# A fused attention and gated feed-forward kernel: the feed-forward's order, its bias and its place among the attention visits

## The chip, the cores and the metric

The kernel runs on one core of one Trainium2 chip. The metric is the device time in microseconds of one execution, the median of several. The profile is one such execution, taken by the hardware profiler; its span runs from the first to the last instruction. The engines are TensorE (PE; its weight loads, PEld, overlap its matmuls), VectorE (DVE), ScalarE (ACT), GpSimd (POOL) and SyncE (SP), whose queue issues most of the DMA transfers here.

## The reference

Eight batches of grouped attention (16 query heads, 4 key heads, 384 positions, head size 64) are followed by a feed-forward with a spatial gate, on each batch's 384 x 1024 attention output.

```python
scores = scale * np.matmul(q, k.transpose(0, 1, 3, 2))
attn = np.exp(scores); attn = attn / (np.sum(attn, axis=-1, keepdims=True) + 1e-09)
x = np.matmul(attn, v)                       # then heads side by side: (8, 384, 1024)
h = np.maximum(x @ w_in, 0.0)                # 1024 -> 1024
u, v = h[..., :512], h[..., 512:]
v_n = (v - mean(v)) / np.sqrt(var(v) + 1e-06)
v_s = np.einsum('ts,bsd->btd', w_spatial, v_n) + b_spatial[None, :, None]
out = (u * v_s) @ w_out                      # 512 -> 1024
```

The bias b_spatial has one value per position t, the same for all 512 channels.

## The kernel before, in words

Matmul operands are fp16, sums are fp32 in PSUM. The 384 positions are three tiles of 128; position s sits in tile s % 3, so that loads are contiguous.

**Attention in visits.** The outer loop (L456) runs over batches b = 0 to 8, the inner one over nine visits vi. Each visit computes two score units (scores, L260; unit u is one 128 x 1024 piece, two matmuls for two heads of 64 rows each, 18 units a batch), and ScalarE takes the exp of each unit into aT (L281). Two PSUM buffers of two banks hold scores, so the scores of one visit wait for the exps of the visit before. At four of the visits (VALUES_AT, L430: visit 0 for the batch before, visits 3, 5 and 8 for the batch itself) values (L285) computes the sums of the exps, their reciprocal on ScalarE (Ln, then Exp with scale -1, L307 and L308), and two pieces X of attention times v, each multiplied by the reciprocal on VectorE into xT (L312). So xT of batch b is complete after visit 0 of batch b+1.

**Feed-forward in pieces.** feed_forward(b) (L418) lists pieces of TensorE work, each with a cost in microseconds that the planner uses: mk_v three times (eight matmuls of 512 columns, relu on ScalarE into v_r, statistics on VectorE; the third also computes rstd on ScalarE and the three v_n on VectorE), mk_u four times (eight matmuls of 384 columns into a transposed U, relu on VectorE into uT, L371), mk_sp four times (a matmul of the bias rows, L380, and three matmuls of v_n with the transposed spatial weights, L382; VectorE multiplies by uT into gT, L389), and mk_out six times (four matmuls of 512 columns, a copy on VectorE, L410; every second one a store of 512 KB, L412).

**The bias as a matmul.** load_bias (L165) splits the 384 biases into an fp16 high part and an fp16 rest, in rows 0 and 32 of bias_rows; bias_ones has ones in these two rows. Their product adds the bias to every channel with fp32-like accuracy.

**The planner.** The pieces of batch b-1 are queued at visit 2 of batch b (L478), or all at once when b is 8 (the tail). In each visit a budget grows by per_visit, the cost of a batch's pieces and four values calls over nine visits, and pieces are taken from the queue while less has been done than the budget allows (L486). In a middle batch that gives V, V, V at visit 2; U at 3; U, U at 4; U at 5; the four spatial pieces at 6; three out at 7, one at 8, two at visit 0 of the next batch; none at visit 1. For the first batch three transposes of the spatial weights (transpose_ws, L209) are put in ahead of the spatial pieces.

**What fixes the order.** TensorE, GpSimd and SyncE run in the order in which the program is written (manual_schedule, L437); VectorE's and ScalarE's order is chosen by the framework's scheduler when the kernel is built. Each engine works in order. One PSUM pool of four banks (ps, L73) is shared in turn by all pieces but the scores: sums, X, V, U, spatial and out. SyncE's queue carries the loads of the next batch (issued in visit 2), the DMA transposes of k and q (visits 6 and 8, after GpSimd's casts to fp16), and the out stores, in the written order.

Of the kernel before, what the change touches and what calls it, by code (L numbers as in the profile page):

```python
# [10 lines left out]
FP32 = mybir.dt.float32  # L11
FP16 = mybir.dt.float16
# [6 lines left out]
def kernel(  # L19
# [20 lines left out]
    P = 128  # L40
# [105 lines left out]
    ident16 = cst.tile([P, P], FP16, name="ident16")  # L146
    ones32 = cst.tile([P, 32], FP16, name="ones32")
    eps_t = cst.tile([P, 1], FP32, name="eps_t")
    bias_rows = cst.tile([P, S], FP16, name="bias_rows")
    bias_ones = cst.tile([P, P], FP16, name="bias_ones")  # L150
    w_in16 = wpool.tile([P, NKT, DFF], FP16, name="w_in16")
    w_out16 = wpool.tile([P, NDT, DM], FP16, name="w_out16")
    wsT16 = wpool.tile([P, NST, S], FP16, name="wsT16")
# [1 line left out]
    def load_consts():  # L155
        make_identity(nc, ident)
        nc.vector.tensor_copy(ident16, ident)  # L157
        nc.vector.memset(ones32, 1.0)
        nc.vector.memset(eps_t, eps_ln)
        nc.vector.memset(bias_rows, 0.0)  # L160
        nc.vector.memset(bias_ones, 0.0)
        nc.vector.memset(bias_ones[0:1, :], 1.0)
        nc.vector.memset(bias_ones[32:33, :], 1.0)

    def load_bias():  # L165
        b32 = cst.tile([1, S], FP32, name="b32")
        lo32 = cst.tile([1, NST, P], FP32, name="lo32")
        nc.sync.dma_start(b32, moe_b_spatial.rearrange("(a s) -> a s", a=1))
        b_tp = b32.rearrange("a (p t) -> a t p", t=NST)
        hi = bias_rows[0:1, :].rearrange("a (t p) -> a t p", t=NST)  # L170
        lo = bias_rows[32:33, :].rearrange("a (t p) -> a t p", t=NST)
        nc.vector.tensor_copy(hi, b_tp)
        nc.vector.tensor_tensor(lo32, b_tp, hi, ALU.subtract)
        nc.vector.tensor_copy(lo, lo32)

    def load_w_in(c0, c1):

# [31 lines left out]
    def transpose_ws(st):  # L209
        ws16 = loaded["ws16"]  # L210
        psw = ps.tile([P, NST, P], FP16, name=f"psw_{st}", tag="ps")
        for tt in range(NST):
            nc.tensor.transpose(psw[:, tt, :], ws16[:, tt, st, :], ident16)
        nc.vector.tensor_copy(wsT16[:, st, :].rearrange("p (t q) -> p t q", t=NST), psw)
# [104 lines left out]
    def mk_v(b, st):  # L319
        def f():  # L320
            xt = xT[b]
            if st == 0:
                held["mv", b] = small.tile([P, NST, 2], FP32, name=f"mv_{b}", tag="mv")
            mv = held["mv", b]
            pv = ps.tile([P, 512], FP32, name=f"pv_{b}_{st}", tag="ps")
            for kc in range(NKT):
                nc.tensor.matmul(  # L327
                    pv,
                    xt[:, kc, st * P : (st + 1) * P],
                    w_in16[:, kc, DH:DFF],  # L330
                    start=(kc == 0),
                    stop=(kc == NKT - 1),
                )
            v_r = moe_v.tile([P, DH], FP32, name=f"v_r_{b}_{st}", tag="v_r")
            nc.scalar.activation(v_r, pv, AF.Relu)
            stats = small.tile([P, 6], FP32, name=f"stats_{b}_{st}", tag="stats")
            nc.vector.bn_stats(stats, v_r)
            nc.vector.bn_aggr(mv[:, st, :], stats)  # L338
            held["v_r", b, st] = v_r
            if st == NST - 1:  # L340
                rstd = small.tile([P, NST], FP32, name=f"rstd_{b}", tag="rstd")
                nc.scalar.activation(rstd, mv[:, :, 1], AF.Ln, bias=eps_t)
                nc.scalar.activation(rstd, rstd, AF.Exp, scale=-0.5)
                for s2 in range(NST):
                    v_n = moe_v.tile([P, DH], FP16, name=f"v_n_{b}_{s2}", tag="v_n")
                    nc.vector.tensor_scalar(
                        v_n,
                        held["v_r", b, s2],
                        mv[:, s2, 0:1],
                        rstd[:, s2 : s2 + 1],  # L350
                        op0=ALU.subtract,
                        op1=ALU.mult,
                    )
                    held["v_n", b, s2] = v_n

        return f

    def mk_u(b, mu):
        def f():
            if mu == 0:  # L360
                held["uT", b] = moe_sb.tile([P, NDT, S], FP16, name=f"uT_{b}", tag="uT")
            pu = ps.tile([P, 512], FP32, name=f"pu_{b}_{mu}", tag="ps")
            for kc in range(NKT):
                nc.tensor.matmul(  # L364
                    pu[:, 0:S],
                    w_in16[:, kc, mu * P : (mu + 1) * P],
                    xT[b][:, kc, :],
                    start=(kc == 0),
                    stop=(kc == NKT - 1),
                )  # L370
            nc.vector.tensor_scalar(held["uT", b][:, mu, :], pu[:, 0:S], 0.0, None, op0=ALU.max)  # L371

        return f

    def mk_sp(b, m):
        def f():
            if m == 0:
                held["gT", b] = moe_sb.tile([P, NDT, S], FP16, name=f"gT_{b}", tag="gT")
            psp = ps.tile([P, 512], FP32, name=f"psp_{b}_{m}", tag="ps")
            nc.tensor.matmul(psp[:, 0:S], bias_ones, bias_rows, start=True, stop=False)  # L380
            for st in range(NST):
                nc.tensor.matmul(  # L382
                    psp[:, 0:S],
                    held["v_n", b, st][:, m * P : (m + 1) * P],
                    wsT16[:, st, :],
                    start=False,
                    stop=(st == NST - 1),
                )
            nc.vector.tensor_tensor(  # L389
                held["gT", b][:, m, :], psp[:, 0:S], held["uT", b][:, m, :], ALU.mult  # L390
            )

        return f
# [23 lines left out]

    def feed_forward(b):  # L418

        return (  # L420
            [(1.72, mk_v(b, st)) for st in range(NST)]
            + [(1.30, mk_u(b, mu)) for mu in range(NDT)]
            + [(0.66, mk_sp(b, m)) for m in range(NDT)]
            + [(0.87, mk_out(b, tt, h)) for tt in range(NST) for h in range(2)]
        )


# [9 lines left out]
    with tc.manual_schedule(engines={PE, POOL, SP}):  # L437
        load_k(0)
        load_q(0, 0, pieces=2)
        cast_k(0, nc.vector)  # L440
        cast_q(0, 0, nc.vector)
        load_v(0)
        load_q(0, 1, pieces=2)
        cast_v(0, nc.gpsimd)
        cast_q(0, 1, nc.gpsimd)
        load_w_in(DH, DFF)
        load_w_in(0, DH)
        load_w_out()
        transpose_k(0)
        transpose_q(0, 0, 0)  # L450
        transpose_q(0, 0, 1)

        total = sum(t for t, _ in feed_forward(0))
        per_visit = (total + 4 * T_VALUES) / VISITS
        budget = 0.0
        for b in range(B + 1):  # L456
            for vi in range(VISITS if b < B else 1):
                if b < B:
                    scores(b, [2 * vi, 2 * vi + 1])
                if vi in VALUES_AT:  # L460
                    db, gp, quad = VALUES_AT[vi]
                    if 0 <= b + db < B and (b < B or db < 0):
                        values(b + db, gp, quad)
                        done += T_VALUES
                if b < B:
                    if b == 0 and vi in (1, 2):
                        transpose_q(b, 1, vi - 1)
                    if vi == 2 and b + 1 < B:
                        load_batch(b + 1, nc.vector if b == 0 else nc.gpsimd)
                    if vi == 6 and b + 1 < B:  # L470
                        dma_transpose_k(b + 1)
                        dma_transpose_q(b + 1, 0)
                    if vi == 8 and b + 1 < B:
                        dma_transpose_q(b + 1, 1)
                    if b == 0 and vi == 3:
                        load_ws()
                        load_bias()
                if vi == 2 and b > 0 or b == B:  # L478
                    queue += feed_forward(b - 1)
                    if b == 1:  # L480
                        queue[7:7] = [(0.2, lambda st=st: transpose_ws(st)) for st in range(NST)]
                if b == 0:
                    done = budget = 0.0
                    continue
                budget += per_visit
                while queue and (b == B or done < budget):  # L486
                    t, f = queue.pop(0)
                    f()
                    done += t
                if not queue:  # L490
                    done = max(done, budget - per_visit)
# [30 lines left out]
```

## Time and profile before

The median of three runs is 290.3 us (289.22 to 290.8). The profiled execution took 289.11 us with a span of 287.3 us, mean granted TensorE clock 0.979.

| stretch of the span (us) | what | length |
|---|---|---|
| 0 to 41.17 | first batch's attention, weights loaded, to the first V matmul | 41.17 |
| 41.17 to 74.68 | first V to second V | 33.51 |
| 74.68 to 235.35 | five middle periods: 32.13, 31.82, 31.83, 32.55, 32.34 | 160.67 |
| 235.35 to 264.28 | last attention visits | 28.93 |
| 264.28 to 287.3 | tail: the last batch's feed-forward and last store | 23.02 |

A stretch between two V matmuls holds one batch of steady work. In the answers of the trace, x after a group is its number of instructions, and an arrow in square brackets names what ended an engine's idle time and how long that was. DMA transfers are busy for 53.6% of 16 engines' span on SyncE's queues and 7.9% on GpSimd's. Duration columns of matmuls overlap, since matmuls are pipelined: the spacing of their starts is what one costs.

### The profile page before, as it was taken

Reading aid. Unit: us, or ns where it says so; the run is one execution under the profiler, and the core shown is the slowest. Engines: PE = TensorE matmul, PEld = TensorE weight load, DVE = VectorE, ACT = ScalarE, POOL = GpSimd, SP = SyncE. Lnnn points to the kernel's source line nnn. Section 1 sums busy time; section 2 is a strip of 40 time slices with the busy share of each in tenths; the row PEclk is TensorE's granted clock in tenths of the full one; section 3 lists DMA queues with packets and bytes.
Section 4 is the critical chain, followed back from the end, with each engine's and each line's share of the span. In section 5 each row is a group of like instructions: output and inputs, shape, how many; then the busy total and the mean of one; then the engine's idle time right before and its main releaser. Section 6 shows DMA issues by size and latency. Waiting matters only on the chain.

```text
span 287.3 us, 5420 instructions
## 1 busy us (share of the span) xinstructions
PE 255.2 (89%) x2247; PEld 113.3 (39%) x2247; DVE 143.8 (50%) x277; ACT 184.4 (64%) x249; POOL 54.0 (19%) x88
## 2 busy tenths in 40 slices
PE   0685879989899989999899989999899989999993
PEld 0431234444344334444344434443344434444551
DVE  3427116474365443574365434674365434575673
ACT  1485895757676686758676776658676786664300
POOL 0654870600140004200150003300150000000000
PEclk9998599999999999999999999999999999999998
DMA  7999999906691479709790549406790530003105
GB/s 215 331 252 124 147 142 216 287 20 198 203 260 29 112 157 312 108 0 203 227 248 13 130 160 329 70 2 202 241 245 2 128 148 0 2 29 121 73 0 219
DMA packets 59402, 42.42 MB, mean 148 GB/s; under 512 B 29041, under 2 KB 55666, under 8 KB 59378
## 3 DMA queue, kind: packets, MB, share of 16 engines
q1 hardware_dynamic: 56274, 38.94, 53.6%
q0 software_dynamic: 3104, 3.15, 7.9%
q8 instruction: 17, 0.28, 0.4%
q14 instruction: 7, 0.06, 0.1%
HBM read 25.76 MB, written 12.58 MB: 133 GB/s over the span
## 4 chain that ended last, share of the span: by engine, by line
PE 75%; ACT 11%; DMA 6%; DVE 4%; issue 1%; SPq 1%; POOL 0%
DMA ws_318<-in_moe_w_spatial_dram 4%; DMA q_0_1_136<-in_q_dram 3%; ACT aT_1_337 L281 1%; ACT aT_0_2652 L281 1%; ACT aT_0_2216 L281 1%; ACT aT_0_471 L281 1%; ACT aT_0_1780 L281 1%; ACT aT_0_1344 L281 1%; ACT aT_0_3088 L281 1%; ACT aT_0_908 L281 1%; ACT aT_1_3288 L281 1%; ACT aT_1_686 L281 1%; SPq L106 1%; DVE ws_320 L204 1%; PE pv_0_3166 L327 1%
## 5 line engine op out<-in xcount | busy, mean ns | idle before, releaser
L364 PEld LDWEIGHTS <-w_in_107 128*128 128x128 f16 x256 | 23.4, 98 | 22.8 <-issue 8.8
L188 POOL DMA_DIRECT2D w_in_107<-in_moe_w_in_dram x32 | 17.2, 544 | 8.1 <-DMA w_in_107<-in_moe_w_in_dram 8.1
L296 PEld LDWEIGHTS <-ones_103 128*32 128x32 f16 x384 | 7.4, 97 | 15.8 <-issue 14.1
L238 PE MATMUL pk_178<-ident_102,k_0_128 128*128 128x128 f16 x6 | 0.8, 303 | 8.4 <-DVE ident_102 L157 8.4
L281 ACT ACTIVATE aT_0_210<-sc_0_204 128x1024 f16<-128x1024 f32 x1 | 1.0, 1023 | 9.1 <-PE sc_0_204 L268 9.1
L268 PEld LDWEIGHTS <-kT_185 64*128 64x128 f16 x36 | 2.1, 103 | 10.9 <-issue 10.8
L116 POOL CAST k_5_1861<-k_5_1857 128x384 f16<-128x384 f32 x2 | 1.0, 507 | 24.3 <-DMA k_5_1857<-in_k_dram 24.3
L116 POOL CAST k_6_2297<-k_6_2293 128x384 f16<-128x384 f32 x2 | 1.0, 507 | 24.1 <-DMA k_6_2293<-in_k_dram 24.1
L116 POOL CAST k_4_1425<-k_4_1421 128x384 f16<-128x384 f32 x2 | 1.0, 508 | 23.5 <-DMA k_4_1421<-in_k_dram 23.5
L116 POOL CAST k_7_2733<-k_7_2729 128x384 f16<-128x384 f32 x2 | 1.0, 508 | 23.4 <-DMA k_7_2729<-in_k_dram 23.4
L296 PEld LDWEIGHTS <-v_0_139 128*32 128x32 f16 x96 | 3.2, 122 | 5.0 <-issue 4.2
L116 POOL CAST k_3_989<-k_3_985 128x384 f16<-128x384 f32 x2 | 1.0, 507 | 20.6 <-DVE mv_1004 L338 20.6
L380 PEld LDWEIGHTS <-bias_ones 128*128 128x128 f16 x32 | 3.1, 97 | 4.3 <-issue 2.7
L204 DVE CAST ws_320<-ws_318 128x384 f16<-128x384 f32 x3 | 1.9, 672 | 5.7 <-DMA ws_318<-in_moe_w_spatial_dram 5.7
L238 PEld LDWEIGHTS <-k_0_128 128*128 128x128 f16 x6 | 0.6, 133 | 8.3 <-DVE k_0_128 L116 4.6
L312 DVE TENSOR_TENSOR xt_273<-X_1_0_0_435,rec_1_0_432 128x384 f16<-128x384 f32 x1 | 0.6, 558 | 6.5 <-ACT rec_1_0_432 L308 6.5
L327 PEld LDWEIGHTS <-xt_3225 128*128 128x128 f16 x24 | 2.4, 98 | 2.8
L403 PEld LDWEIGHTS <-gT_3644 128*128 128x128 f16 x24 | 2.3, 98 | 3.0 <-DVE gT_3644 L389 0.5
L327 PEld LDWEIGHTS <-xt_624 128*128 128x128 f16 x24 | 2.3, 98 | 2.8 <-issue 0.2
L327 PEld LDWEIGHTS <-xt_2808 128*128 128x128 f16 x24 | 2.3, 98 | 2.8 <-issue 0.2
L327 PEld LDWEIGHTS <-xt_2372 128*128 128x128 f16 x24 | 2.3, 98 | 2.8 <-issue 0.2
L327 PEld LDWEIGHTS <-xt_273 128*128 128x128 f16 x24 | 2.3, 98 | 2.8 <-issue 0.2
(1077 smaller groups left out, 755.9 us busy)
## 6 DMA issues: line engine op xcount, KB each, us to landing
w_in_107<-in_moe_w_in_dram POOLq DMA_DIRECT2D x32, 64.0 KB, 5.4
w_out_108<-in_moe_w_out_dram POOLq DMA_DIRECT2D x2, 512.0 KB, 7.8
q_0_0_125<-in_q_dram SPq DMA_DIRECT2D x2, 384.0 KB, 4.9
q_0_1_136<-in_q_dram SPq DMA_DIRECT2D x2, 384.0 KB, 7.5
q_1_0_248<-in_q_dram SPq DMA_DIRECT2D x1, 768.0 KB, 6.6
q_1_1_258<-in_q_dram SPq DMA_DIRECT2D x1, 768.0 KB, 8.5
q_2_0_536<-in_q_dram SPq DMA_DIRECT2D x1, 768.0 KB, 7.7
q_2_1_546<-in_q_dram SPq DMA_DIRECT2D x1, 768.0 KB, 7.8
```

The lines of the kernel that those rows point to most:

```text
L106: nc.sync.dma_start(q32[:, i * n : (i + 1) * n, :], q[b, h0 : h0 + n].rearrange("h (p t) d -> p h (t d)", t=NST),)
L116: engine.tensor_copy(k16[:, gp], k32[:, gp])
L188: nc.gpsimd.dma_start(w_in16[32 * i : 32 * (i + 1), kc : kc + 2, c0:c1], rows[jq])
L204: nc.vector.tensor_copy(ws16[:, tt, :, :], ws32[:, tt, :].rearrange("p (s t) -> p t s", t=NST))
L238: nc.tensor.transpose(pk[:, gp, t, :], k16[:, gp, t, :, :].rearrange("p h d -> p (h d)"), ident16,)
L268: nc.tensor.matmul(sc[:, half, :], kT[b][lo:hi, gp, t, :], rhs[lo:hi, c * 512 : (c + 1) * 512], start=True, stop=True,)
L281: nc.scalar.activation(aT[b, gp][:, t, :, c * 512 : (c + 1) * 512], sc, AF.Exp, scale=scale)
L296: nc.tensor.matmul(dst[32 * i : 32 * (i + 1), 0:S], weights(t, half), a[:, t, half, j * S : (j + 1) * S], start=(t == 0), stop=(t == NST - 1),
L327: nc.tensor.matmul(pv, xt[:, kc, st * P : (st + 1) * P], w_in16[:, kc, DH:DFF], start=(kc == 0), stop=(kc == NKT - 1),)
L364: nc.tensor.matmul(pu[:, 0:S], w_in16[:, kc, mu * P : (mu + 1) * P], xT[b][:, kc, :], start=(kc == 0), stop=(kc == NKT - 1),)
L380: nc.tensor.matmul(psp[:, 0:S], bias_ones, bias_rows, start=True, stop=False)
L403: nc.tensor.matmul(po, gT[:, m, tt * P : (tt + 1) * P], w_out16[:, m, half * 512 : (half + 1) * 512], start=(m == 0), stop=(m == NDT - 1),)
```

## The change

The feed-forward's order becomes V, out of the batch before, spatial, U; the last batch's own out follows at the end. Spatial no longer needs U: it writes v_s with the bias added, in fp32, on VectorE, from a bias that a DMA has laid out over all 128 partitions (bias_b). U's evacuation then does relu and the product with v_s in one VectorE instruction, straight into gT. So the bias matmul, the bias rows and uT go; v_s (fp32) comes. Out of batch b-1 takes U's place between V and spatial, as work for TensorE while VectorE and ScalarE normalise V. The pieces are queued from visit 1 on instead of visit 2, and the planner's total becomes 17.58 instead of 18.22. The batch of the first feed-forward has no earlier out; it gets the three small transposes of the spatial weights in that place.

```diff
-    bias_rows = cst.tile([P, S], FP16, name="bias_rows")
-    bias_ones = cst.tile([P, P], FP16, name="bias_ones")
+    bias_b = cst.tile([P, S], FP32, name="bias_b")
...
-        nc.vector.memset(bias_rows, 0.0)
-        nc.vector.memset(bias_ones, 0.0)
-        nc.vector.memset(bias_ones[0:1, :], 1.0)
-        nc.vector.memset(bias_ones[32:33, :], 1.0)
 
     def load_bias():
...
-        nc.sync.dma_start(b32, moe_b_spatial.rearrange("(a s) -> a s", a=1))
...
-        nc.vector.tensor_copy(hi, b_tp)
-        nc.vector.tensor_tensor(lo32, b_tp, hi, ALU.subtract)
-        nc.vector.tensor_copy(lo, lo32)
+        nc.sync.dma_start(bias_b, moe_b_spatial.partition_broadcast(P))
...
+    def mk_sp(b, m):
+        def f():
+            if m == 0:
+                held["v_s", b] = moe_sb.tile([P, NDT, S], FP32, name=f"v_s_{b}", tag="v_s")
+            psp = ps.tile([P, 512], FP32, name=f"psp_{b}_{m}", tag="ps")
+            for st in range(NST):
+                nc.tensor.matmul(
+                    psp[:, 0:S],
+                    held["v_n", b, st][:, m * P : (m + 1) * P],
+                    wsT16[:, st, :],
+                    start=(st == 0),
+                    stop=(st == NST - 1),
+                )
+            nc.vector.tensor_tensor(
+                held["v_s", b][:, m, :].rearrange("p (t s) -> p t s", t=NST),
+                psp[:, 0:S].rearrange("p (t s) -> p t s", t=NST),
+                bias_b.rearrange("p (s t) -> p t s", t=NST),
+                ALU.add,
+            )
...
     def mk_u(b, mu):
...
-            nc.vector.tensor_scalar(held["uT", b][:, mu, :], pu[:, 0:S], 0.0, None, op0=ALU.max)
...
-            nc.tensor.matmul(psp[:, 0:S], bias_ones, bias_rows, start=True, stop=False)
...
-            nc.vector.tensor_tensor(
-                held["gT", b][:, m, :], psp[:, 0:S], held["uT", b][:, m, :], ALU.mult
-            )
+            nc.vector.scalar_tensor_tensor(
+                held["gT", b][:, mu, :],
+                pu[:, 0:S],
+                0.0,
+                held["v_s", b][:, mu, :],
+                op0=ALU.max,
+                op1=ALU.mult,
+            )
...
     def feed_forward(b):
 
+        last = [(0.87, mk_out(b - 1, tt, h)) for tt in range(NST) for h in range(2)] if b else []
+        own = [(0.87, mk_out(b, tt, h)) for tt in range(NST) for h in range(2)] if b == B - 1 else []
         return (
             [(1.72, mk_v(b, st)) for st in range(NST)]
+            + (last or [(0.2, lambda st=st: transpose_ws(st)) for st in range(NST)])
+            + [(0.50, mk_sp(b, m)) for m in range(NDT)]
             + [(1.30, mk_u(b, mu)) for mu in range(NDT)]
-            + [(0.66, mk_sp(b, m)) for m in range(NDT)]
-            + [(0.87, mk_out(b, tt, h)) for tt in range(NST) for h in range(2)]
+            + own
         )
...
-        total = sum(t for t, _ in feed_forward(0))
+        total = sum(t for t, _ in feed_forward(1))
...
-                if vi == 2 and b > 0 or b == B:
+                if vi == 1 and b > 0 or b == B:
                     queue += feed_forward(b - 1)
-                    if b == 1:
-                        queue[7:7] = [(0.2, lambda st=st: transpose_ws(st)) for st in range(NST)]
```

More of the change, by code (lines that the diff above doesn't have):

```diff
@@ L159, in load_consts @@
         nc.vector.memset(eps_t, eps_ln)
-        nc.vector.memset(bias_rows, 0.0)
-        nc.vector.memset(bias_ones, 0.0)
-        nc.vector.memset(bias_ones[0:1, :], 1.0)
-        nc.vector.memset(bias_ones[32:33, :], 1.0)
     def load_bias():
-        b32 = cst.tile([1, S], FP32, name="b32")
-        lo32 = cst.tile([1, NST, P], FP32, name="lo32")
-        nc.sync.dma_start(b32, moe_b_spatial.rearrange("(a s) -> a s", a=1))
[L169 to L172, printed above, removed]
-        nc.vector.tensor_tensor(lo32, b_tp, hi, ALU.subtract)
-        nc.vector.tensor_copy(lo, lo32)
+        nc.sync.dma_start(bias_b, moe_b_spatial.partition_broadcast(P))
     def load_w_in(c0, c1):
@@ L356, in mk_v @@
         return f
+    def mk_sp(b, m):
[17 more added lines that the diff above has]
+            )
+        return f
     def mk_u(b, mu):
@@ L360, in f @@
             if mu == 0:
-                held["uT", b] = moe_sb.tile([P, NDT, S], FP16, name=f"uT_{b}", tag="uT")
+                held["gT", b] = moe_sb.tile([P, NDT, S], FP16, name=f"gT_{b}", tag="gT")
             pu = ps.tile([P, 512], FP32, name=f"pu_{b}_{mu}", tag="ps")
@@ L370, in f @@
                 )
-            nc.vector.tensor_scalar(held["uT", b][:, mu, :], pu[:, 0:S], 0.0, None, op0=ALU.max)
[L373 to L387, printed above, removed]
-                )
-            nc.vector.tensor_tensor(
-                held["gT", b][:, m, :], psp[:, 0:S], held["uT", b][:, m, :], ALU.mult
+            nc.vector.scalar_tensor_tensor(
[5 more added lines that the diff above has]
+                op1=ALU.mult,
             )
```

## The prediction

> **What bounds the kernel now.** First the page's busy rows and the chain that ended last.
>
> ```profile
> PE 255.2 (89%) x2247; PEld 113.3 (39%) x2247; DVE 143.8 (50%) x277; ACT 184.4 (64%) x249; POOL 54.0 (19%) x88
> PE 75%; ACT 11%; DMA 6%; DVE 4%; issue 1%; SPq 1%; POOL 0%
> ```
>
> TensorE is busy 89% of the span and is 75% of the chain; ScalarE is 11% of it. So a matmul removed is time removed, as long as ScalarE isn't waited for. I cut the span at the first V matmul of each batch (their starts are in the chain) and asked for busy time per stretch; three of the eight:
>
> ```profile
> 41.17:74.68 33.51, 31.32 (x286) 14.04 (x287) 17.19 (x34) 23.02 (x32) 4.92 (x7) 1.00 0.77 172
> 106.81:138.63 31.82, 30.40 (x277) 13.38 (x278) 16.14 (x31) 22.85 (x32) 4.93 (x7) 1.00 0.66 155
> 264.28:287.30 23.02, 18.33 (x97) 9.12 (x94) 13.09 (x24) 2.29 (x5) 0.00 (x0) 0.96 0.23 94
> ```
>
> Columns: stretch and length, then PE, PEld, DVE, ACT, POOL, clock, DMA. A middle batch lasts 31.82 us. VectorE (16.14) and ScalarE (22.85) have room over a whole batch; the lost time must be local. The timeline around a batch's first V matmul shows where:
>
> ```profile
> 103.99 0.39 PE L268 MATMUL sc_2_1405<-qT_0_1221,kT_1219 64*128 64x512 f16 x2
> 104.42 1.02 ACT L281 ACTIVATE aT_0_1344<-sc_2_1405 128x1024 f16<-128x1024 f32 x1 [1.07 <-PE sc_2_1405 L268]
> 105.34 1.02 ACT L281 ACTIVATE aT_0_1344<-sc_3_1408 128x1024 f16<-128x1024 f32 x1
> 105.50 0.39 PE L268 MATMUL sc_4_1413<-qT_0_1221,kT_1219 64*128 64x512 f16 x2 [0.90 <-ACT aT_0_1344 L281]
> 106.41 0.39 PE L268 MATMUL sc_5_1416<-qT_0_1221,kT_1219 64*128 64x512 f16 x2 [0.52 <-ACT aT_0_1344 L281]
> 106.74 1.90 PE L327 MATMUL pv_0_1441<-w_in_107,xt_1064 128*128 128x512 f16 x8
> ...
> 122.85 0.34 PE L380 MATMUL psp_0_1660<-bias_rows,bias_ones 128*128 128x384 f16 x1
> 123.02 0.33 PE L382 MATMUL psp_0_1660<-wsT_109,v_n_0_1486 128*128 128x384 f16 x1
> ```
>
> Visit 1 has no feed-forward piece. Its two score units only fill the two score buffers, so visit 2's units wait for exps: without the waits V would begin 0.45 us (two units) and 0.09 us (switch) after 104.45, at 104.99, and it begins at 106.8: 1.83 us lost per batch (same gaps from 136.27 to 138.63). The bias matmul takes 123.02 - 122.85 = 0.16 us. Last, the chain in the first batch:
>
> ```profile
> 22.64 1.86 DVE ws_320 L204 x3
> 24.49 0.57 DVE bias_rows L172
> 25.68 0.55 DVE xt_273 L312
> 26.27 1.15 PE X_0_1_1_377 L296 x12
> ```
>
> TensorE waits for xt_273 while VectorE prepares the bias rows.
>
> [...] gT (L389) measures 0.557. [...] the bias is read at stride 3. [...] ws_320's cast reads 384 fp32 at stride 3 and takes 0.65. [...] v_n_1_2360 takes 1.04 us instead of 0.54 beside a GpSimd cast. [...] the trace shows clock 0.50 from 28 to 36 us.
>
> **The change, part by part.**
>
> *Bias matmuls.* 32 x 0.163 = 5.2 us off TensorE, 0.65 per batch, all on the chain.
>
> *Bias rows.* The three small VectorE operations go; those before xt_273 span 24.49 to 25.68, so 1.19 us off the chain. Four memsets at the start lie inside the wait for the first loads: nothing. The broadcast load (128 rows of 1.5 KB) runs behind ws and is needed near 47 us: nothing.
>
> *VectorE.* Per batch, four relus (0.55) and four products (0.557) become four adds and four gated evacuations. Neither is in the trace: low bound 0.557, high 0.67 (the strided cast). I take 0.56; at 0.67 it is 8 x 0.11 = 0.9 us more on an engine with 15 us free per batch, hidden by U's 1.30 us per piece. Spatial pieces take 0.49 each on TensorE, less than their add, but four PSUM buffers and U follow.
>
> *Order and visit.* Following the queue arithmetic, a middle batch now does: visit 1 V V V out; 2 out x3; 3 values, out; 4 out, sp x3; 5 values, sp, U; 6 U U; 7 U; 8 values; 0 values. As many switches as before (20). So TensorE without waits needs 31.82 - 1.83 - 0.65 = 29.34 us. The light visits are now 7, 8 and 0, so I replay the waits there with the trace's spacings (exp to exp 0.92, exp start to release 1.07, exp to Ln 0.90, Ln to Exp 0.53, Exp to multiply 0.56, score to exp 0.43), t=0 at visit 7's scores. Visit 7: exps start 0.43 and 1.35. Visit 8: its second unit waits for the release at 2.42, wanted 2.17: 0.25 lost; values end 4.21; exps 2.37 and 3.29, Ln 4.19, Exp 4.72. Visit 0: scores at 4.30 wait for nothing, values end 6.39, 0.05 lost on a PSUM buffer; exps 5.24, 6.16, Ln 7.06, Exp 7.59. Visit 1: its second unit waits for 7.23, wanted 6.71: 0.52; V starts 7.55, its eighth matmul at 9.06 waits for the multiply done at 9.22: 0.16. Sum 0.98.
>
> Then the added wait. In the built order VectorE has v_n behind two out copies and before two others, po_1_0 and po_1_1; ScalarE computes rstd between visit 2's exps. V ends 12.90, relu 13.7, stats and aggregate 15.24, rstd Ln 15.27, exp, rstd Exp 16.49, v_n 16.72 to 18.1, copy of po_1_0 done 18.8. Visit 3's X needs that PSUM buffer at 18.61: about 0.2, with the next out 0.27. Visit 5's U waits 0.15 for sums' Ln. Spatial comes at 22.1, after v_n: out(b-1) hides that chain as U did. Total 0.98 + 0.27 + 0.15 = 1.40, so 30.74 a batch; before, an otherwise equal batch took 0.31 more than the best (32.13), so I take 31.0.
>
> *DMA.* The stores' queue is in order: they come at visits 2 to 4 now, and the DMA transposes of k and q queue behind the third store, at t=23 instead of soon after the cast. They issue over 8 us (2.0 + 2.4 + 3.4), land in 5 to 7, so kT and q's first half by about 32.5, needed at 35.3: hidden. Loads follow the transposes without a store ahead of them, so they and GpSimd's casts come some 14 us earlier, no longer beside v_n: the 0.5 to 0.7 us extra of two later batches (32.55, 32.34) should go.
>
> *Stages.*
> First V: 37.3. Now it follows visit 2's scores at 41.17. In the new order it follows visit 1's: values end at 37.81 - 1.19 = 36.6, the second unit's buffer is released at 36.94 + 1.07 - 1.19 = 36.8, so both units are done at 37.2. The multiplies that V's last two matmuls need end near 38.3 and 38.8, just in time. So 1.19 us come from the bias rows, 2.7 from the visit. The V half of w_in is there: by 32.6 loads had been issued that wait for its last pieces.
> First period: V to 42.5, scores, nine small transposes to 43.65; spatial then waits for v_n, since only 0.6 us of transposes stand in for out: relu 43.26, two exps, Ln 45.1, v_n from 45.7 to 47.2, so 3 us idle. Behind that piece on TensorE stand a second spatial piece and visit 3's scores, and ScalarE, its exps done at 45.1, waits for these. Visit 3 to 51.1, 4 to 54.5, 5 to 58, 6 to 60; then visits 7, 8, 0 run at ScalarE's pace, V at 67.5: 30.2, against 33.51 (it has no out).
> Five middle periods: 155.0 against 160.67.
> Last period: 31.0 less visits 0 and 1's scores and exp waits, 1.65: 29.35 against 28.93.
> Tail: V 5.19, out 5.19, sp 1.96, U 5.2, out 5.2 = 22.74, plus 1.0 (v_n ahead of the out copies, then sp's four adds, delay PSUM buffers) and 0.17 (last gate), 23.9; after the last matmul 4.66 as now: 28.55 against 23.02.
> Sum 37.3 + 30.2 + 155.0 + 29.35 + 28.55 = 280.4 against the 287.3 span, -6.9. From the median 290.3: 283.4 us.
>
> **Rivals.**
> *The moved out is paid in full.* The last batch carries 5.2 us more, and the first period, bound by ScalarE, gives little back. For: its 3 us stall, and light visits 7 to 0. If the stall halves the clock for 3.4 us or more and light visits cost more, it is 33 instead of 30.2: 286.4 us.
> *v_n in front of the copies.* If rstd falls one exp later (0.92) in every batch, TensorE stands at visit 3: 7 x 0.92 = 6.4, so 289.8, no change. For: strict order on ScalarE and VectorE; against: I find 0.3.
> *Slower: transposes late.* In the first batch qT_0 took 14.5 us to land. If so behind the stores, it lands at 39.5 instead of before 35.3: 4.2 x 6 = 25, so 308; half of that, 296. Against: then the weights shared the DMA; here loads have moved away.
> *Better.* No 0.25 extra per batch and a short first stall: 281.
>
> **How the numbers follow.** Forecast (282 to 285) 0.52, moved out paid 0.22, better 0.13, v_n 0.07, late transposes 0.06. The predicted time is the forecast's. Range 280.8 to 287.6: it takes in the second case and most of the better one, leaving out the last two and tails. Faster by over 0.5% (below 288.85): 0.52 + 0.22 + 0.13 = 0.87 and a little of v_n is offset by tails; within 0.5% 0.07; slower 0.06.
>
> **What would show it.** Right: no bias_rows; middle periods near 31.0; waits of sc_17 and sc_3 on exps summing to about 0.8 in place of sc_4's and sc_5's 1.4; first V near 37; a wait of about 3 us of the first spatial piece on v_n; casts before v_n. Wrong: sc_0 waiting on a DMA, X at visit 3 waiting over 0.5 us, clock below 1.0 after 43 us, adds above 0.7 us.

## The result, and the profile after

The changed kernel takes 280.33 us (median of 4 runs, 278.88 to 281.92) against 289.76 us for the kernel before on the same chip: ratio 0.968, 95% interval 0.961 to 0.975. That is 9.4 us less. The prediction had 6.9 less and 283.4 us, with a range from 280.8; the result lies half a microsecond under it. The kernel before itself came at 289.8 here and not at the 290.3 from which the forecast started.

The page's busy rows and the shares of the chain that ended last, after:

```profile
PE 251.8 (91%) x2215; PEld 110.6 (40%) x2215; DVE 139.7 (50%) x270; ACT 184.0 (66%) x249; POOL 53.9 (19%) x88
PE 69%; ACT 19%; DMA 7%; DVE 1%; issue 1%; SPq 1%; POOL 0%
```

TensorE has 32 matmuls fewer (2215) and is still the bound; ScalarE holds more of the chain, 19% instead of 11%. Busy time per stretch, from V to V: the first period, a middle one and the tail (stretch and length, then PE, PEld, DVE, ACT, POOL, clock, DMA):

```profile
36.14:67.68 31.54, 27.48 (x259) 11.78 (x259) 13.45 (x28) 22.71 (x32) 11.74 (x18) 0.95 1.05 193
98.23:128.77 30.54, 30.18 (x273) 13.05 (x274) 16.23 (x31) 22.82 (x32) 5.12 (x8) 1.00 0.59 164
250.00:277.80 27.80, 23.12 (x116) 11.07 (x116) 16.83 (x31) 2.30 (x5) 0.00 (x0) 0.95 0.28 114
```

A middle batch went from 31.82 to 30.54, and its idle TensorE from 1.42 to 0.36. The five middle periods are now even (30.54 or 30.55 each); before they ran from 31.82 to 32.55. Ahead of V, the timeline shows what is left of the waits, now at visits 8, 0 and 1 (sc_16 and sc_17 are visit 8's scores, sc_0 and sc_1 visit 0's, sc_2 and sc_3 visit 1's):

```profile
123.19 0.39 PE L255 MATMUL sc_16_1670<-qT_1_1290,kT_1196 64*128 64x512 f16 x2
123.67 0.39 PE L255 MATMUL sc_17_1673<-qT_1_1290,kT_1196 64*128 64x512 f16 x2
...
125.57 0.39 PE L255 MATMUL sc_0_1724<-qT_0_1630,kT_1628 64*128 64x512 f16 x2
125.80 0.38 PE L255 MATMUL sc_1_1727<-qT_0_1630,kT_1628 64*128 64x512 f16 x2
...
127.75 0.39 PE L255 MATMUL sc_2_1777<-qT_0_1630,kT_1628 64*128 64x512 f16 x2
128.38 0.39 PE L255 MATMUL sc_3_1780<-qT_0_1630,kT_1628 64*128 64x512 f16 x2 [0.24 <-ACT aT_0_1730 L268]
128.71 2.06 PE L314 MATMUL pv_0_1786<-w_in_106,xt_1468 128*128 128x512 f16 x8
130.60 1.89 PE L314 MATMUL pv_1_1800<-w_in_106,xt_1468 128*128 128x512 f16 x8
132.33 1.89 PE L314 MATMUL pv_2_1814<-w_in_106,xt_1468 128*128 128x512 f16 x8
```

The idle time listed at sc_3 is 0.24 us, where sc_4 and sc_5 had 0.90 and 0.52. Durations overlap, so the starts say more. Two score units that wait for nothing start 0.22 us apart (sc_0 and sc_1); sc_17 comes 0.25 later than that and sc_3 0.40. V's first eight matmuls take 1.89 from start to start and the next eight 1.73, because the eighth waits 0.15 for its multiply. By the same measure sc_4 and sc_5 of the kernel before lost 1.05 and 0.69. At the start, the weight cast is followed by the multiplies at once, with no bias rows between:

```profile
22.91 1.84 DVE L191 CAST ws_315<-ws_313 128x384 f16<-128x384 f32 x3 [6.07 <-DMA ws_313<-in_moe_w_spatial_dram]
...
24.67 0.55 DVE L299 TENSOR_TENSOR xt_268<-X_0_0_0_285,rec_0_0_282 128x384 f16<-128x384 f32 x1
...
25.27 0.67 PE L283 MATMUL X_0_1_1_367<-aT_0_205,v_0_134 128*32 128x384 f16 x12 [1.44 <-DVE xt_268 L299]
```

X_0_1_1 starts at 25.27 instead of 26.27. Last, the stall in the first period, where no out stands between V and spatial, and the scores behind it:

```profile
45.12 0.34 PE L351 MATMUL psp_0_611<-wsT_108,v_n_0_562 128*128 128x384 f16 x1 [2.37 <-DVE v_n_0_562 L333]
...
46.94 0.61 PE L255 MATMUL sc_6_621<-qT_0_391,kT_389 64*128 64x512 f16 x2
```

The two score matmuls take 0.61 instead of 0.39: the granted clock was 0.50 from 46.56 to 49.97. X_0_0_1 at 49.80 is the last slow one.

The stages against the prediction's sum, in us (tail: from the last V to the end):

| stage | before | predicted | after |
|---|---|---|---|
| first V | 41.17 | 37.3 | 36.14 |
| first period | 33.51 | 30.2 | 31.54 |
| five middle periods | 160.67 | 155.0 | 152.73 |
| last period | 28.93 | 29.35 | 29.59 |
| tail | 23.02 | 28.55 | 27.80 |
| span | 287.3 | 280.4 | 277.8 |

The span is 2.6 below the forecast, and 2.3 of that lie in the middle periods.

### The profile page after: what moved, and what is told of

The parts are those of the page before. It is cut to its first block, busy times and chain, and to the rows that moved or that the text cites. A ratio compares the mean times of both kernels' runs of the same rounds, so it can differ in the third digit from the quotient of the medians.

```text
span 277.8 us, 5353 instructions
## 1 busy us (share of the span) xinstructions
PE 251.8 (91%) x2215; PEld 110.6 (40%) x2215; DVE 139.7 (50%) x270; ACT 184.0 (66%) x249; POOL 53.9 (19%) x88
## 4 chain that ended last, share of the span: by engine, by line
PE 69%; ACT 19%; DMA 7%; DVE 1%; issue 1%; SPq 1%; POOL 0%
DMA ws_313<-in_moe_w_spatial_dram 4%; DMA q_0_1_131<-in_q_dram 3%; ACT aT_1_691 L268 2%; ACT aT_1_2823 L268 1%; ACT aT_1_3236 L268 1%; ACT aT_1_2391 L268 1%; ACT aT_1_1527 L268 1%; ACT aT_1_1095 L268 1%; ACT aT_1_1959 L268 1%; ACT aT_1_327 L268 1%; PE pv_0_517 L314 1%; PE pv_0_1786 L314 1%; PE pv_0_1354 L314 1%; PE pv_0_3082 L314 1%; PE pv_0_2650 L314 1%
## 5 line engine op out<-in xcount | busy, mean ns | idle before, releaser
L283 PEld LDWEIGHTS <-ones_103 128*32 128x32 f16 x384 | 7.6, 98 | 14.1 <-issue 12.3
L255 PEld LDWEIGHTS <-kT_180 64*128 64x128 f16 x36 | 2.0, 99 | 10.5 <-issue 10.2
L116 POOL CAST k_7_2720<-k_7_2716 128x384 f16<-128x384 f32 x2 | 1.0, 510 | 22.9 <-DMA k_7_2716<-in_k_dram 22.9
L116 POOL CAST k_6_2288<-k_6_2284 128x384 f16<-128x384 f32 x2 | 1.0, 509 | 22.3 <-issue 22.3
L116 POOL CAST k_5_1856<-k_5_1852 128x384 f16<-128x384 f32 x2 | 1.0, 509 | 22.2 <-issue 22.2
L283 PEld LDWEIGHTS <-v_0_134 128*32 128x32 f16 x96 | 3.1, 117 | 4.0 <-issue 3.2
L116 POOL CAST k_4_1424<-k_4_1420 128x384 f16<-128x384 f32 x2 | 1.0, 509 | 17.1 <-issue 17.1
L283 PEld LDWEIGHTS <-v_1_255 128*32 128x32 f16 x96 | 2.9, 108 | 1.8 <-issue 0.8
L283 PEld LDWEIGHTS <-v_7_2730 128*32 128x32 f16 x96 | 2.6, 96 | 2.1 <-issue 0.7
```

The costliest lines, as they stand in the source:

```text
L116: engine.tensor_copy(k16[:, gp], k32[:, gp])
L255: nc.tensor.matmul(sc[:, half, :], kT[b][lo:hi, gp, t, :], rhs[lo:hi, c * 512 : (c + 1) * 512], start=True, stop=True,)
L283: nc.tensor.matmul(dst[32 * i : 32 * (i + 1), 0:S], weights(t, half), a[:, t, half, j * S : (j + 1) * S], start=(t == 0), stop=(t == NST - 1),
```

## Experiments

My theory: the move to visit 1 and the bias matmuls bring what there is, and the moved out is paid in full in the tail. The rival: the order itself brings part of it, by what it hides. On the miss, two candidates: the margin of 0.26 per middle batch was a cost of GpSimd casts beside v_n that the change takes away, or the new order hides waits that I priced. The diffs of this section are shortened to the lines that matter.

**Only the bias matmuls away** (kernel before; the bias is left out of the result).

```diff
-            nc.tensor.matmul(psp[:, 0:S], bias_ones, bias_rows, start=True, stop=False)
-                    start=False,
+                    start=(st == 0),
```

> The kernel before without the 32 bias matmuls (the result leaves the bias out); the bias rows are still prepared. If the matmuls lie on the path at full price: 32 x 0.163 = 5.2 us less, 284.6 us (ratio 0.982), middle periods 0.65 us shorter. Rival, exp waits take up the room: the wait before V grows and only some 2 us come off, ratio 0.993.

283.76 us, ratio 0.981 (0.977 to 0.985). Four of the five middle periods are 31.18 (the fifth 31.51), which is 31.83 less 0.65: each removed matmul is worth its 0.163 us on the path, as priced.

**Only the visit** (kernel before, queued from visit 1).

```diff
-                if vi == 2 and b > 0 or b == B:
+                if vi == 1 and b > 0 or b == B:
```

> The kernel before with its feed-forward queued from visit 1, nothing else. The planner's arithmetic then leaves only visit 0 without a piece (it has values), so the exp waits of 1.83 us a middle period should shrink to about 0.1: first V at about 38.4, middle periods 30.1, total near 274 to 276 (ratio 0.95), below the changed kernel although the bias matmuls are still there. Rival, the place of the queue only moves the waits as in the changed kernel (about 1 us a period stay) and gains 2.7 at the start and 0.8 a period: 282 (ratio 0.974). Second rival, the visit is worth nothing: 290.

279.67 us, ratio 0.968 (0.961 to 0.974). This one character gives as much as the whole change. The windows of a middle period and of the tail:

```profile
71.55:102.23 30.68, 30.61 (x277) 13.23 (x278) 16.39 (x31) 22.85 (x32) 4.93 (x7) 1.00 0.64 162
254.58:277.70 23.12, 18.44 (x97) 9.16 (x96) 13.41 (x25) 2.32 (x6) 0.00 (x0) 0.96 0.22 91
```

TensorE is busy 30.61 of 30.68 us with the bias matmuls still in, and the tail stays at 23.12. I had expected 274 to 276, with periods of 30.1. By the starts of its matmuls 0.47 us of short waits are left in such a period, which the overlapping durations cover (V's eighth matmul 0.15, out's fourth 0.24, scores 0.08), and 30.2 stay without them, where I had put 29.99.

**The change without the visit** (kernel after, queued from visit 2).

```diff
-                if vi == 1 and b > 0 or b == B:
+                if vi == 2 and b > 0 or b == B:
```

> The changed kernel queued from visit 2 again. Visit 1 is then empty, and visits 8 and 0 light. If the visit matters as the replay has it: first V 2.7 us later, middle periods about 31.4 instead of 30.55, total near 286.5. If the gain comes from order and bias alone: 280 to 281.

295.03 us, ratio 1.020 (1.015 to 1.025): slower than before, and far above the 286.5 that I had expected. So in the new order the visit is worth about 15 us (0.968 against 1.020), more than the 9.4 that it brings in the old one. The score waits of 1.46 and 0.52 are back in front of V. Three of its five middle periods lasted 31.9 and two 33.6, with the same waits. The timeline of V at the start of one of each kind:

```profile
105.57 0.39 PE L255 MATMUL sc<-qT,kT 64*128 64x512 f16 x2 [0.52 <-ACT aT L268]
105.89 5.35 PE L314 MATMUL pv<-w_in,xt 128*128 128x512 f16 x24
...
137.45 0.39 PE L255 MATMUL sc<-qT,kT 64*128 64x512 f16 x2 [0.52 <-ACT aT L268]
137.78 7.04 PE L314 MATMUL pv<-w_in,xt 128*128 128x512 f16 x24
```

The same 24 matmuls take 7.04 in place of 5.35: from 138 to 141.3 the granted clock was 0.50. So behind the same 2 us of waits three batches paid 1.7 more, the last among them, which explains some 5 us of the miss.

**The change without the bias part** (kernel after, with bias rows and bias matmul, v_s a plain copy).

```diff
+            nc.tensor.matmul(psp[:, 0:S], bias_ones, bias_rows, start=True, stop=False)
-            nc.vector.tensor_tensor(v_s[m], psp, bias_b, ALU.add)
+            nc.vector.tensor_copy(v_s[m], psp)
```

> The changed kernel with the bias added by a matmul again (bias rows prepared as before), v_s evacuated by a plain copy. If the bias part of the change is worth its price: 5.2 us of matmuls and 1.2 to 2.4 at the start (bias rows, clock) come back, 287 to 288. If exp waits hide part of the matmuls: 283 to 285.

284.92 us, ratio 0.985 (0.981 to 0.989). So the change splits, along this path and by ratios of 289.6 us: the visit -9.4 (1 to 0.968), the order +5.1 (0.968 to 0.985, this run against the visit alone), the bias part -5.1 (0.985 to 0.968). The order's cost is where the theory put it: the tail is 28.3 here against 23.1 with the visit alone. The first period gives 2.3 back (30.34 against 32.66), and the middle periods take most of it again, at 31.02 against 30.68. In the new order the bias matmuls are worth 0.48 a middle period (31.02 to 30.54) and not 0.65: without them U at visit 5 waits 0.19 us for its PSUM buffer, and with them it doesn't.

**Bias rows later** (kernel before, rows prepared at visit 8).

```diff
-                        load_bias()
+                    if b == 0 and vi == 8:
+                        load_bias()
```

> The kernel before with only its bias rows loaded and prepared five visits later, out of VectorE's way in front of the first attention multiplies. Theory: 1.2 us off the chain at the start, [...] together 1.5 to 3 us: first V at 38 to 39.7, the rest as before, 286 to 287.5. Rival, ScalarE sets the pace there and nothing comes: first V at 41.

289.49 us, ratio 1.001 (0.999 to 1.003): no gain. The rows were not removed but moved in front of something else, as VectorE's timeline shows:

```profile
49.52 0.67 DVE L172 CAST bias_rows<-b 1x384 f16<-1x384 f32 x1 [1.78 <-DMA b<-in_moe_b_spatial_dram]
...
52.27 0.63 DVE L346 TENSOR_SCALAR v_n<-v_r,mv,rstd 128x512 f16<-128x512 f32 x1
```

The first V came 0.7 earlier (40.44) although the weight cast began 0.8 later, with 10.2 us of half clock ahead of it as in the kernel before, and the first period took 34.6 instead of 33.5, since the rows' load now held VectorE before v_n. The run says that this place is no better, not that the rows were free.

**Loads earlier** (kernel before, the next load written at visit 0 instead of 2).

```diff
-                    if vi == 2 and b + 1 < B:
+                    if vi == (0 if b else 2) and b + 1 < B:
```

> The kernel before with the next batch's loads written at visit 0 instead of 2 (from the second batch on), ahead of a batch's third store in the queue, so GpSimd's casts come some 3.6 us earlier and no longer beside v_n. Theory: the middle periods of 32.13, 32.55 and 32.34 fall to 31.82, v_n to 0.55 us each, 1.5 us in all (ratio 0.995). Rival: the 0.3 to 0.7 us have another cause and stay.

288.19 us, ratio 0.9945 (0.992 to 0.997). Periods that had been 32.13 and 32.55 are 31.82 now. One of 32.16 remains, and in it GpSimd's cast lies beside v_n:

```profile
209.62 1.88 POOL L128 CAST q<-q 128x768 f16<-128x768 f32 x2 [2.49 <-issue]
210.27 1.96 DVE L346 TENSOR_SCALAR v_n<-v_r,mv,rstd 128x512 f16<-128x512 f32 x3 [1.58 <-ACT rstd L343]
```

Three v_n take 1.96 where they take 1.46 without a cast beside them (in the run with casts held to v_n). So the 0.3 to 0.7 that set some of before's batches apart was the cost of casts beside v_n.

**The change with a pause** (kernel after, an empty piece of 2.6 in the queue ahead of the first spatial, so that the first wait for v_n falls behind more attention).

```diff
+ [(2.6, lambda: None)]   # first batch only, behind the weight transposes
```

> The changed kernel with an empty piece of cost 2.6 in the first feed-forward between the weight transposes and spatial, so that spatial begins two visits later and finds v_n ready. Theory: the wait of 2.4 us on v_n and the half clock after it go, the first period falls from 31.5 to 28 or 29, total 277 to 278.5. Rival: ScalarE has no work left to bring forward and the pieces pushed to later visits cost the same, 280.

280.7 us, not told apart from the change: two of its four times were 276.6 and 278.7, the others 282.7 and 282.9. In the trace of the 278.7 the stall on v_n is gone, but in its place the scores wait 2.55 us for qT's DMA transpose. The granted clock stays at 1.00 all the same, and the first period is 29.3 us instead of 31.54. The first V came at 37.5.

**Casts held to v_n** (kernel after, a tiny GpSimd copy that reads the first v_n, written ahead of the casts; in the trace it ran at 109.07 and they followed it).

```diff
+                    if s2 == 0:
+                        nc.gpsimd.tensor_copy(mark, v_n[:, 0:8])
```

> The kernel after, with a tiny GpSimd copy of 8 columns of v_n's first tile, written when v_n is: GpSimd's queue is in order, so the casts of the next load start only there, beside the other two v_n, as they lay in some batches of before. Theory (the 0.31 between 31.82 and 32.13 of before was this contention, and is the margin that the prediction added a second time): v_n at some 1.0 in place of 0.54, middle periods 30.85 to 31.0, span up by 1.5 to 2.3 from 277.8, ratio 0.974. Rival (out's pieces hide a later v_n, so a longer v_n costs nothing, and the margin was too large for another reason): middle periods 30.55, span 277.8, ratio 0.968.

280.25 us, ratio 0.966 (0.962 to 0.971). The run missed its aim: the casts began at 109.46, after the third v_n had begun (109.4), and each v_n stayed at 0.54. Middle periods were 30.54 to 30.61. What it does show: casts beside the copies of out cost at most 0.06.

**Casts held to rstd** (the same, half a microsecond earlier).

```diff
+                nc.gpsimd.tensor_copy(mark, rstd)
                 for s2 in range(NST):
```

> As the run that held GpSimd's casts to v_n, but the tiny GpSimd copy now reads rstd, which is ready before the first v_n: there the mark ended and the casts began only as the third v_n ended (109.46 against 109.92), v_n stayed at 0.54, and a period lengthened by 0.06 (30.61). Now the casts begin half a us earlier, beside the second and third v_n. Theory (the 0.31 of before's 32.13 was a cast beside v_n, and is the margin that the prediction added a second time): at least one v_n of each batch at some 1.0, middle periods 30.85 to 31.05. Rival (a later v_n is hidden in the new order, and the margin would have been too large even beside casts): v_n at 1.0, middle periods 30.55 to 30.65.

282.52 us, ratio 0.976 (0.971 to 0.982). A middle period's window:

```profile
100.83:131.74 30.91, 30.32 (x274) 13.07 (x274) 16.68 (x31) 22.80 (x32) 5.55 (x8) 1.00 0.59 165
```

and, from the timeline inside it, v_n, the casts, and the matmul that waits:

```profile
109.75 1.83 DVE L335 TENSOR_SCALAR v_n<-v_r,mv,rstd 128x512 f16<-128x512 f32 x3 [0.38 <-ACT rstd L330]
...
109.91 1.39 POOL L116 CAST k<-k 128x384 f16<-128x384 f32 x2
...
112.24 0.67 PE L283 MATMUL X<-aT,v 128*32 128x384 f16 x12 [0.23 <-DVE osb L408]
```

The three v_n take 1.83 instead of 1.46, the copy of po_1_0 behind them comes later, and X at visit 3 waits for its buffer: it starts 0.90 after the X before it, where the changed kernel has 0.53. That 0.37 is the whole loss; the period is 30.91, 0.36 longer. With the casts beside v_n the new order would have run within 0.1 of the 31.0 that I forecast; without them it runs at 30.55. (I had expected one v_n of about 1.0; the loss was spread, 0.37 over three.)

**Old order, visit 1, bias added by VectorE and a separate multiply.**

```diff
+            nc.vector.tensor_tensor(v_s, psp, bias_b, ALU.add)
-            nc.vector.tensor_tensor(gT[m], psp, uT[m], ALU.mult)
+            nc.vector.tensor_tensor(gT[m], v_s, uT[m], ALU.mult)
```

> Old order, queued from visit 1, bias added by VectorE: spatial is evacuated into fp32 with the bias added, and a second VectorE instruction multiplies by uT. If visit and bias add up and the new order is what costs: 277.7 span, less 5.2 for the matmuls and 1 to 3 at the start, plus 0.5 to 1.2 a period where out follows spatial within a visit and waits for two VectorE steps instead of one: 272 to 276, below the changed kernel (280). Rival, the gains don't add: 280.

312.2 us (304.77 to 315.67), far off what I expected; even the best time is 25 us above the visit alone. TensorE's mean clock was 0.93 to 0.95. VectorE's timeline shows what out has to wait for:

```profile
128.29 0.66 DVE L376 TENSOR_TENSOR v_s<-psp,bias_b 128x384 f32<-128x384 f32 x1
128.98 0.56 DVE L382 TENSOR_TENSOR gT<-v_s,uT 128x384 f16<-128x384 f32 x1
129.46 1.23 DVE L376 TENSOR_TENSOR v_s<-psp,bias_b 128x384 f32<-128x384 f32 x2
130.60 1.02 DVE L382 TENSOR_TENSOR gT<-v_s,uT 128x384 f16<-128x384 f32 x2
```

Spatial is 2 us of TensorE and now 4.9 us of VectorE, and out, next in the queue, needs all of it: out's matmuls wait 17.1 us for gT over the run, in 21 waits, and middle periods take 34.3 to 36.1 at mean granted clocks of 0.90 to 0.95, for each batch had half clock for 3.4 or 6.8 us. VectorE was busy 18.7 to 19.2 us of each middle period, and this slack average did not hide the adds, with no TensorE work behind them. In the order of the change, U is that work.

**Out back in its own batch, U split around spatial.** This follows from the split above: keep the visit and the add, give up the moved out. The order is V, U 0 and 1 (relu alone), spatial, U 2 and 3 (gated), out.

```diff
-            + (last or [(0.2, lambda st=st: transpose_ws(st)) for st in range(NST)])
-            + [(0.50, mk_sp(b, m)) for m in range(NDT)]
-            + [(1.30, mk_u(b, mu)) for mu in range(NDT)]
-            + own
+        return v + u[:2] + ws + sp + u[2:] + o
# in mk_u: relu alone for mu < 2; with mu == 2 the two products of v_s and uT
```

> The kernel after, with out back in its own batch: order V, U 0 and 1 (relu alone), spatial, U 2 and 3 gated; pieces 0 and 1 get their product by a VectorE multiply written with U 2. Still from visit 1, bias still added by VectorE; nothing is left out. Theory (the moved out is paid in full in the tail, and the bias matmuls are paid per period): first V 37, first period 32.2 (32.66 of the old order at visit 1, less 0.65, plus a little wait), middle periods 30.3, last 29, tail 24.2 (23.1 less 0.65, plus some 1.7 of waits for v_n and for the products): span 274, time 276.3, ratio 0.954. Rival (spatial after only two U pieces waits for v_n in every batch, and out for the products, as out did for the gates with all four products on VectorE): 1 to 1.5 per period, middle 31.3 to 31.8, span 279 to 282, ratio 0.97 to 0.98.

275.85 us (273.83 to 277.75), ratio 0.9515 (0.945 to 0.958), near the expected 276.3, though not by its parts: middle periods are 29.94 or 29.95, below the 30.3 of the theory, and the first period of the trace was longer (see the next run).

**The same, and the last batch as before** (V, U, spatial with the bias matmul, out, so that nothing waits in the tail; the rows are prepared in the last batch's attention).

```diff
+        if b == B - 1:
+            return v + u + sp + o
```

> As the run with out back in its own batch, but the last batch keeps the order of before, V, U, spatial with the bias matmul, product from PSUM, out; the bias rows are prepared during the last batch's attention. Nothing is left out. Theory: as that run up to the last V, tail 23.1 instead of 24.2: span 272.8, time 275.2, ratio 0.951. Rival (the late preparation of the rows, or the waits, cost as much as they save): same as that run within 0.5.

273.07 us (272.63 to 273.21), ratio 0.942 (0.938 to 0.945): faster than both kernels, by 16.5 us than the one before. Its windows of the first period, a middle one and the tail:

```profile
37.02:69.25 32.23, 31.17 (x283) 13.50 (x283) 19.20 (x36) 22.92 (x32) 11.88 (x17) 1.00 0.97 200
69.25:99.19 29.94, 29.93 (x273) 12.78 (x274) 17.79 (x33) 22.86 (x32) 4.92 (x7) 1.00 0.69 165
248.13:271.20 23.07, 18.44 (x96) 9.15 (x96) 13.20 (x25) 2.29 (x5) 0.00 (x0) 0.97 0.23 92
```

A middle batch shows no TensorE idle: 29.93 of 29.94. (By starts, 0.40 of short waits are still in it, under overlapping durations.) The tail is 23.07 instead of 27.80. Against the version before it the tails gain only 0.4 (23.47 there, not the 24.2 that I expected). The profiles differ more in the first period: there the scores waited 3.5 us for qT's transpose, 6.8 us of half clock followed, and the period took 37.4 instead of 32.2. The two programs queue the same work there, so I take it for the timing of the transfers, which no run settles; the wide interval of that version fits it.

## Why the prediction was right and wrong

**The direction and the mechanisms held.** The matmuls were worth 0.163 each on the path in the old order (31.83 to 31.18). The waits came where the replay put them: sc_17 and sc_3 on exps in place of sc_4 and sc_5. Middle batches became even. The transposes were early enough, and in the middle batches no cast of a load ran beside v_n (v_n from 107.16, the casts before it up to 101.2 and the next from 123.42). The add took 0.65 to 0.70 us against the 0.56 taken and the 0.67 given as upper bound (the strided casts that it rests on took 0.65 to 0.69), and TensorE did not wait for it in the middle batches; the gated evacuation took 0.558. "The moved out is paid in full" was the second case and is shown: +5.1 against the visit alone.

**The failed step is the margin of the middle batches**: "before, an otherwise equal batch took 0.31 more than the best (32.13), so I take 31.0". The replay gave 30.74, the margin added 0.26, and 30.55 came. That 0.31 was v_n beside a GpSimd cast, in the trace of before:

```profile
83.03 0.83 POOL L121 CAST v_3_999<-v_3_995 128x768 f16<-128x768 f32 x1
83.12 1.02 DVE L346 TENSOR_SCALAR v_n_0_1050<-v_r_0_1014,mv_1004,rstd_1047 128x512 f16<-128x512 f32 x1 [1.57 <-ACT rstd_1047 L343]
...
83.96 1.47 PE L364 MATMUL pu_1_1129<-xt_624,w_in_107 128*128 128x384 f16 x8
85.57 1.46 PE L364 MATMUL pu_2_1139<-xt_624,w_in_107 128*128 128x384 f16 x8
```

The first v_n takes 1.02 instead of 0.54, the work behind it on VectorE comes later, and the third U piece starts 1.61 after the second, where the best batch has 1.31: the 0.3. It is the very cost of casts beside v_n that the DMA part of the prediction took away from two later batches. The 32.13 was never checked for the same cause, so a cost that the change removes was charged to the changed kernel. The run with casts held to rstd puts it back and finds 30.91; without it there is nothing to charge. The 31.0 stands in five middle periods and, less a subtraction, in the last one. Six times 0.26 is 1.6 us; without it the forecast would have been 281.8, and a range moved down as much would have begun at 279.2. The prediction's own better case, "No 0.25 extra per batch and a short first stall: 281", came nearest to the time, partly by luck: its first half came true, and its second did not, as half clock followed the stall.

**The replay itself held, term by term.** What each wait costs is read from starts, beyond the usual distance of the same two instructions:

| wait in a middle period | replay | measured |
|---|---|---|
| sc_17 on an exp | 0.25 | 0.25 |
| X of visit 0 on a PSUM buffer | 0.05 | 0.04 |
| sc_3 on an exp | 0.52 | 0.40 |
| V's eighth matmul on a multiply | 0.16 | 0.15 |
| X of visit 3 and the next out, behind v_n | 0.27 | 0.02 |
| U of visit 5 on ScalarE's Ln of the sums | 0.15 | 0.19 |
| sum | 1.40 | 1.05 |

The U wait, in the timeline of another batch: U starts 0.36 after the last spatial matmul, where 0.16 is usual, as soon as ScalarE has read the sums:

```profile
146.61 0.50 ACT L294 ACTIVATE rec_0_1_2005<-sums_0_1_1992 128x384 f32<-128x384 f32 x1
146.80 0.33 PE L351 MATMUL psp_3_2036<-wsT_108,v_n_2_1835 128*128 128x384 f16 x1
147.16 1.46 PE L373 MATMUL pu_0_2042<-xt_1468,w_in_106 128*128 128x384 f16 x8
```

Without these waits 29.5 us are left, against 29.34 in the prediction. Most of that difference is the 1.83 of wait taken off the 31.82: by starts, sc_4 and sc_5 had lost 1.74. (V's 106.8 was read from the chain, the other starts from the timeline, where V starts at 106.74.) So the waits were 0.35 too high and the rest about 0.16 too low, and the replay's sum came 0.19 high per batch.

**First V, 36.14 instead of 37.3.** The cast of the spatial weights waits for its load and starts at 22.6 to 24.4 in the traces, so I count from there to V in the kernels that start at visit 1.

| kernels (one trace each) | half clock in between, us | cast to V, us |
|---|---|---|
| the change | 3.4 | 13.2 |
| pause; out in its own batch (two) | 6.8 | 13.6 to 14.2 |
| casts held (two) | 10.2 | 14.7 |
| with bias rows: visit alone; change without the bias part | 10.2 | 15.8 |

At equal half clock the bias rows cost 1.2, as the 1.19 said; these are single traces, and no run set the half clock. From the cast of the trace before (22.64) and with the 10.2 us of half clock that it had, V without rows would stand at 37.3 (an estimate from this table), which is the forecast. So the 1.16 that came on top is the shorter half clock of this trace, which nothing in the prediction foresaw: luck. Why it was shorter is not shown; ahead of it stands a wait for xt of 1.44 instead of 2.38, but the waits of the other kernels don't follow the table's order.

**First period, 31.54 instead of 30.2.** The stall of "about 3 us" was 2.37, and the risk named in the first rival came true: 3.4 us of half clock after it (33 instead of 30.2 makes that case 286.2, not 286.4). In the change without the bias part a stall of 2.2 left the clock at 1.00 and the period took 30.34, with 0.65 of bias matmuls in it. With the pause, a wait of 2.55 elsewhere left the clock at 1.00, and the period took 29.3. In the two kernels with casts held, a stall of 2.4 was followed by half clock too (mean clock 0.94), and the period took 30.84; so 0.7 of the 31.54 has another cause, which stays open.

**Tail, 27.80 instead of 28.55.** From V's start to its last matmul's end at 273.13 TensorE is busy 23.12 of 23.13 us. By starts, some 0.33 of that is waiting: 0.17 for the last gate, as forecast, and 0.16 around spatial and the first U, where I had added 1.0 for v_n and delayed PSUM buffers. The matmuls' 22.74 was right.

Adding up: -1.16, +1.34, -2.27, +0.24, -0.75 make -2.6 on the span. The other 0.5 of the 3.1 us between forecast and median is the start, 290.3 against 289.8. First V and first period nearly cancel, by luck. What is left lies on one side, and the range had no room for it: the margin, the waits of sc_3 and of X behind v_n in the middle batches, and those of the tail.

## What to carry to other kernels

Before a slow sample becomes a margin, look for its cause: if the change removes it, it is not a margin. A window in which TensorE is busy throughout can still hold waits: durations of matmuls overlap, and only the starts show them (0.40 us in a period of 29.94 with 29.93 busy). And where an evacuation grows, give TensorE other work behind it: adds and multiplies directly ahead of out gave middle periods of 34.3 to 36.1 us instead of 30.68; in the order of the change, with U behind the adds, out did not wait for them in the middle batches.

## What the runs showed of the hardware

In the change without the visit, the same waits (1.46 and 0.52) ahead of the same V were followed by a granted clock of 0.50 in three batches of six and by 1.00 in the other three; 3.4 us of half clock cost 1.7. In the changed kernel a stall of 2.37 us was followed by half clock; one of 2.2 in the change without the bias part and one of 2.55 in the change with a pause were not. What decides it is not shown. Ahead of the first V the stretches of half clock lasted 3.4, 6.8 or 10.2 us in the traces, later in the runs 3.4 or 6.8. Such a wait in this kernel has to be priced with both outcomes.

Beside a GpSimd cast, v_n, which reads SBUF, took longer: three in 1.83 to 1.96 instead of 1.46. Casts beside the copies of out, which read PSUM, cost a period no more than 0.06, and two such copies took 1.28 us with casts beside them and without. The bias add with a second operand read at stride 3 took 0.65 to 0.70 us; a multiply of the same size without a stride took 0.56, and U's relu of a PSUM tile of the same size 0.53 to 0.56.
